# Two decoder layers at batch 8: the layer norm taken off the chain between attention and feed-forward, and two visits instead of four placed between the layers

## The chip, the cores and the metric

The kernel runs on one core of one Trainium2 chip. The metric is the time of one execution on the device in microseconds (us); of several executions the median counts. Beside the times there is one execution taken by the hardware profiler, with its own time and its span (first to last instruction).

The engines are called PE (matmul; PEld is its weight load), DVE (vector), ACT (scalar activation), POOL (GpSimd) and SP, the engine whose queue issues all the DMAs here.

## The reference

Eight sequences decode one token each (D = 640). The same attention block and the same feed-forward block are applied twice, with the same weights and the same cache:

```python
x = A_x
x = x + _A_ref(_layernorm(x), k_cache, v_cache, wq, wo)
x = x + _B_ref(_layernorm(x), w1, w2)
x = x + _A_ref(_layernorm(x), k_cache, v_cache, wq, wo)
x = x + _B_ref(_layernorm(x), w1, w2)
```

`_A_ref` is attention with 32 heads of 128 over 4096 cached positions: q = x wq, scores q.k / sqrt(128), softmax, weighted sum of v, output projection wo. `_B_ref` is relu(x w1) w2 with 1728 hidden values. `_layernorm` is (x - mean) / sqrt(var + 1e-5) without weights. Everything is bfloat16. The cache is 8 x 32 x 4096 x 128 elements each for keys and values, 1.07 GB together.

## The kernel before, in words

**Tiles.** A *visit* is one sequence b with one pair of heads hp in one layer: (layer, b, hp). It needs the keys of the pair (K) and its values (V), each in four *units* of 128 partitions x 2048 bf16, 512 KB. The units live in an *arena* of G = 26 places. SP loads one to eight neighbouring units with one DMA (`do_load`, L477).

**Order of the work.** `plan` (L33) writes the whole program out beforehand, as a list of steps. For each sequence it runs 16 visits of layer 0 and, later, 16 of layer 1. The last three pairs of heads in layer 0 are the first three in layer 1, and 21 of their units stay in the arena (`keep`, L59); two more are copied to PSUM and back (`stash`, L60; `do_stash` L464, `do_unstash` L472). So 23 units of a sequence are loaded once instead of twice. Between the last visit of layer 0 of sequence b and its first visit of layer 1 the plan puts the first AHEAD = 4 visits of sequence b + 1 (L43 to L49), since layer 1 can't begin before the feed-forward block is through. While those visits run, the 21 kept units are held and five places are left.

Within the list, K of a visit comes before V of the visit ahead of it (L63 to L65); at the end of a sequence's layer 0 the two are swapped. `feed` (L106) puts a load into the list as soon as places are free, so SP's queue follows the order in which PE frees units (`release`, L137). A load waits on SP until the matmuls that read the old unit are done. Everything else is a *chain*: a list of steps with costs, from which `step` (L159), called after each unit, takes one step of each chain as long as the costs stay within CAP = 20. `until` (L168) runs a chain forward to a step that is needed now. The engines' queues follow this list in order; nothing is reordered later.

**One visit.** Scores: 64 matmuls with the cache as weights (L524). Then the row maximum (M1, L530), across partitions (T L534, M2 L538, B L543), exponentials on ACT (E, L545: a maximum with the scale -1/sqrt(128), and Exp with the scale 1/sqrt(128)), sums (L556, I), the product with V (L512), its copy on ACT (OC, L570), gathering (OG, L575), division by the sum (O, L585), output projection with 10 matmuls (W, L592), and the addition to x on DVE (Y, L601). Layer 1 does W for all eight sequences at once, at the end.

**The end of a layer** (`finish`, L178, and `finish_steps`, L404). After Y of the last visit the chain has these steps: sums of x over its five columns (DVE), mean (a fp32 matmul with ones), center (subtract, square, reduce, on DVE), var (a fp32 matmul), scale. In layer 0, scale calls `inverse_root` (L386): one operation on DVE and eleven on POOL, then one more on POOL (L375) that writes the normalized row. Two empty steps follow. Then come five steps `up` (70 matmuls with w1, L417), relu on ACT (L425, L428), five steps `down` (70 matmuls with w2, L434), add. In layer 0 the same norm follows for layer 1, and then the queries of the first two pairs (Q L496, QC on ACT L504); each further query is made two visits ahead. Layer 1's end, done once for all sequences, takes the root with Sqrt on ACT (L380) and a reciprocal on DVE instead.

The pieces of the plan that set this:

```python
visits += nxt[:AHEAD] + cur + nxt[AHEAD:]
norm = [(0, "sums"), (2, "mean"), (0, "center"), (2, "var"), (0, "scale"), (1, None), (1, None)]
c = norm + [(15, ("up", k)) for k in range(n_up)] + [(0, "relu")]
c += [(14, ("down", k)) for k in range(n_down)] + [(0, "add")]
if layer == 0:
    c += norm
```

Of the kernel before, what the change touches and what calls it, by code (L numbers as in the profile page):

```python
# [16 lines left out]
UNIT = 4  # L17
# [5 lines left out]
AHEAD = 4  # L23
# [9 lines left out]
def plan(B, NP, n_up, n_down):  # L33
# [29 lines left out]
    for i in range(NV + 1):  # L63
        pair = [("K", i)] * (i < NV) + [("V", i - 1)] * (i >= 1)
        slots += pair[::-1] if i and visits[i - 1][0] == 0 and last_of[visits[i - 1][:2]] == i - 1 else pair  # L65
    stream = []
    for which, i in slots:
        layer, b, hp = visits[i]
        stream += [(which, i, g) for g in range(UNIT) if layer == 0 or (which, hp, g) not in keep]
# [7 lines left out]
    weights.setdefault(max(1, NP - 4), []).append(("w2",))  # L77

# [16 lines left out]
    def place(x):  # L95

        if visits[x[1]][0] and stashed(*x) is not None:
            return None, stashed(*x), False
        return visits[x[1]][1], tile_at(NP, x[0], visits[x[1]][2]) * UNIT + x[2], keeps(*x)
# [6 lines left out]
    def feed():  # L106

        while at[0] < len(stream):
# [4 lines left out]
            while n < most and b is not None and place(stream[at[0] + n]) == (b, p + n, keeping):  # L113
                n += 1
# [10 lines left out]
            if b is None:  # L125
                lands[u] = clock[0] + 2
                ops.append(("unstash", p, u))
                continue
# [8 lines left out]
    def release(which, i, g):  # L137
        key = which, visits[i][1], visits[i][2], g
        u = where.pop((which, i, g), None)
        if key in kept:  # L140
            if visits[i][0] == 0:
                return
            u = kept.pop(key)
        if visits[i][0] == 0 and stashed(which, i, g) is not None:
            ops.append(("stash", stashed(which, i, g), u))
        at[1] += 1
        owner[u], freed[u] = False, at[1]
        feed()
# [29 lines left out]
    def finish(layer, b):  # L178

        norm = [(0, "sums"), (2, "mean"), (0, "center"), (2, "var"), (0, "scale"), (1, None), (1, None)]  # L180
        c = norm + [(15, ("up", k)) for k in range(n_up)] + [(0, "relu")]
        c += [(14, ("down", k)) for k in range(n_down)] + [(0, "add")]
        if layer == 0:
            c += norm
        c = [(n, op and ("C", layer, b, k, op)) for k, (n, op) in enumerate(c)]
        if layer == 0:
            c += query(b, 0) + query(b, 1)
# [3 lines left out]
    for which, i in slots:  # L191
# [18 lines left out]
        if which == "K":  # L210
            ops.append(("M1", i))
# [3 lines left out]
        else:  # L215
            until(("I", i))
            ops.append(("OC", i))
            step()
            chains.append([(6, ("OG", i)), (0, ("O", i))])
            if layer == 0 or b == B - 1:  # L220
                chains[-1] += [(10, ("W", i)), (0, ("Y", i))]
            if last_of[layer, b] == i and (layer == 0 or b == B - 1):
                chains[-1] += finish(layer, b)
# [16 lines left out]
def kernel(  # L240
# [82 lines left out]
    for c in range(4):  # L323
        rows = slice(32 * c, 32 * c + CJ)
        nc.vector.tensor_copy(out=gsel[rows, :, c // 2], in_=ident[rows, rows])
    eps_c = consts.tile([P, 1], FP32, name="eps_c")
# [19 lines left out]
    def ln_steps(b0, nb, xln, key):  # L346
        x = xT[:, b0 : b0 + nb, :]

        def sums():
            s1 = st[key, "s1"] = sm.tile([P, nb], FP32, name="s1", bufs=1)  # L350
            nc.vector.tensor_reduce(out=s1, in_=x, axis=AX.X, op=ALU.add)

        def mean():
            st[key, "mean"] = oy_ps[:, 64 : 64 + nb]
            nc.tensor.matmul(st[key, "mean"], lhsT=ones_f, rhs=st[key, "s1"], start=True, stop=True)

        def center():
            xc = st[key, "xc"] = sm.tile([P, nb, DC], FP32, name="xc", bufs=1)
            nc.vector.scalar_tensor_tensor(
                out=xc, in0=_free(st[key, "mean"], [(1, nb), (0, DC)]), scalar=-1.0 / D, in1=x, op0=ALU.mult, op1=ALU.add  # L360
            )
            sq = sm.tile([P, nb, DC], FP32, name="sq", bufs=1)
            nc.vector.tensor_tensor(out=sq, in0=xc, in1=xc, op=ALU.mult)
            s2 = st[key, "s2"] = sm.tile([P, nb], FP32, name="s2", bufs=1)
            nc.vector.tensor_reduce(out=s2, in_=sq, axis=AX.X, op=ALU.add)

        def var():
            st[key, "var"] = oy_ps[:, 72 : 72 + nb]
            nc.tensor.matmul(st[key, "var"], lhsT=ones_f, rhs=st[key, "s2"], start=True, stop=True)

        def scale():
            rstd = sm.tile([P, nb], FP32, name="rstd", bufs=1)
            if nb == 1:
                inverse_root(rstd, st[key, "var"])
                nc.gpsimd.tensor_scalar(  # L375
                    out=xln[:, 0, :], in0=st[key, "xc"][:, 0, :], scalar1=rstd, scalar2=None, op0=ALU.mult
                )
            else:
                std = sm.tile([P, nb], FP32, name="std", bufs=1)
                nc.scalar.activation(out=std, in_=st[key, "var"], func=ACT.Sqrt, bias=eps_c, scale=1.0 / D)  # L380
                nc.vector.reciprocal(out=rstd, in_=std)
                nc.vector.tensor_tensor(out=xln, in0=st[key, "xc"], in1=_free(rstd, [(1, nb), (0, DC)]), op=ALU.mult)

        return dict(sums=sums, mean=mean, center=center, var=var, scale=scale)

    def inverse_root(out, s2):  # L386
# [3 lines left out]
        nc.vector.tensor_scalar(out=v[:, 0:1], in0=s2, scalar1=1.0 / D, scalar2=eps, op0=ALU.mult, op1=ALU.add)  # L390
# [12 lines left out]

    def finish_steps(layer, b):  # L404


        b0, nb = (b, 1) if layer == 0 else (0, B)
        xf = sm.tile([P, nb, DC], BF16, name="xf", bufs=1)
        key = layer, b

        def up(k):
            if k == 0:
                st[key, "h"] = oy_ps[:, 128 : 128 + FC * nb].rearrange("p (f b) -> p f b", b=nb)
            for f in up_parts[k]:
                fs = f_sizes[f]
                for c in range(DC):
                    nc.tensor.matmul(  # L417
                        st[key, "h"][:fs, f, :], lhsT=w1_sb[:, c, f * P : f * P + fs], rhs=xf[:, :, c],
                        start=(c == 0), stop=(c == DC - 1),
                    )  # L420

        def relu():
            hT = st[key, "hT"] = sm.tile([P, FC, nb], BF16, name="hT", bufs=1)
            if n_full:
                nc.scalar.activation(out=hT[:, :n_full], in_=st[key, "h"][:, :n_full], func=ACT.Relu)  # L425
            if Dff % P:
                rem = Dff % P
                nc.scalar.activation(out=hT[:rem, n_full:], in_=st[key, "h"][:rem, n_full:], func=ACT.Relu)  # L428

        def down(c):  # L430
            if c == 0:
                st[key, "y"] = oy_ps[:, 256 : 256 + DC * nb].rearrange("p (c b) -> p c b", b=nb)
            for f, fs in enumerate(f_sizes):
                nc.tensor.matmul(  # L434
                    st[key, "y"][:, c, :], lhsT=w2_sb[:fs, f, c * P : (c + 1) * P],
                    rhs=st[key, "hT"][:fs, f, :], start=(f == 0), stop=(f == FC - 1),
                )

        def add():
            dst = xT if layer == 0 else outT  # L440
            nc.vector.tensor_tensor(
                out=dst[:, b0 : b0 + nb, :], in0=xT[:, b0 : b0 + nb, :],
# [229 lines left out]
```

## Time and profile before

| what | value |
|---|---|
| time, median of 3 runs | 2374.44 us (2373.16 to 2378.14) |
| the profiled execution's own time | 2376.09 us |
| its span | 2374.3 us, 57948 instructions |
| busy: PE, PEld | 1292.5 us (54%), 783.7 us (33%) |
| busy: DVE, ACT, POOL | 377.7 us (16%), 355.9 us (15%), 42.8 us (2%) |
| moved by DMA | 996.04 MB, mean 420 GB/s |
| read from HBM | 992.27 MB |
| loads of the cache | 632 DMAs: 348 of 1 unit, 35 of 2, 17 of 3, 100 of 4, 16 of 5, 6 of 6, 1 of 7, 109 of 8 |

How to read the profile: the page gives the busy time of each engine, then the span in 40 slices with DMA share and rate, then the chain of waits followed back from the last instruction, then groups of instructions and the DMA issues with their time from issue to landing. A view by stages gives the same figures for any stretch of the span; a timeline lists the instructions in order, with, in brackets, how long the engine was idle before each and what released it. The DMA share is the time in which packets were under way on the core's 16 DMA engines.

### The profile page before, as it was taken

How to read it: one execution, taken by the hardware profiler on the slowest of the kernel's cores; microseconds unless marked ns; L12 is line 12 of the kernel's file. 1: busy time of each engine (PE TensorE's matmuls, PEld its weight loads, DVE VectorE, ACT ScalarE, POOL GpSimd, SP SyncE). 2: the span in 40 equal slices, each digit the busy share in tenths (PEclk: the TensorE clock that was granted, in tenths of full speed). 3: DMA queues.
4: the chain of work that ended last, by engine and by line, in shares of the span. 5: the costliest groups of instructions: out<-in, count | busy, mean ns of one | idle time of the engine just before them, and what ended most of it. 6: DMA issues, size and time to landing. Idle time of an engine off the chain costs nothing.

```text
span 2374.3 us, 57948 instructions
## 1 busy us (share of the span) xinstructions
PE 1292.5 (54%) x26486; PEld 783.7 (33%) x26486; DVE 377.7 (16%) x1840; ACT 355.9 (15%) x1195; POOL 42.8 (2%) x198
## 2 busy tenths in 40 slices
PE   3436644476445754458454574446744466545845
PEld 2324322243223532225222352223422244223523
DVE  1102111121111211112111121112211112112211
ACT  1111211111111211112111121111211112111211
POOL 0000000000000000000000000000000000000000
DMA  9999999999999999999999999999999999999997
GB/s 411 428 429 403 428 432 431 429 398 433 428 433 427 391 433 428 433 423 404 430 434 433 406 401 431 433 431 408 420 431 430 430 408 417 431 432 410 405 434 302
DMA packets 92794, 996.04 MB, mean 420 GB/s; under 512 B 10372, under 2 KB 10372, under 8 KB 54916
## 3 DMA queue, kind: packets, MB, share of 16 engines
q1 hardware_dynamic: 92548, 992.33, 99.1%
q8 instruction: 207, 3.39, 0.5%
q14 instruction: 39, 0.32, 0.0%
HBM read 992.27 MB, written 0.01 MB: 418 GB/s over the span
## 4 chain that ended last, share of the span: by engine, by line
DMA 81%; PE 14%; DVE 2%; ACT 2%; issue 1%; POOL 1%; SPq 0%; POOLq 0%; DVEq 0%; ACTq 0%
DMA arena<-in_A_kv_dram 81%; PE o_ps L512 5%; PE s_ps L524 5%; ACT o_sb L570 1%; DVE hmx L538 1%; PE oy_ps L575 1%; PE blk_ps L496 1%; PE blk_ps L543 1%; DVE diag L540 0%; PE oy_ps L592 0%; PE blk_ps L534 0%; PE oy_ps L434 0%; DMA wq_sb<-in_A_wq_dram 0%; DVE arena L475 0%; POOL root L399 0%
## 5 line engine op out<-in xcount | busy, mean ns | idle before, releaser
L512 PE MATMUL o_ps<-arena,P_sb 128*4 128x512 bf16 x4096 | 564.8, 599 | 373.9 <-DMA arena<-in_A_kv_dram 371.6
L524 PEld LDWEIGHTS <-arena 128*128 128x128 bf16 x16384 | 501.6, 105 | 667.0 <-DMA arena<-in_A_kv_dram 660.7
L524 PE MATMUL s_ps<-q_96,arena 128*128 128x1 bf16 x8192 | 275.2, 166 | 371.9 <-DMA arena<-in_A_kv_dram 360.0
L547 ACT ACTIVATE nmax<-blk_ps 128x2 f32<-128x2 f32 x256 | 44.0, 172 | 1638.3 <-PE blk_ps L543 1638.3
L512 PEld LDWEIGHTS <-P_sb 128*4 128x4 bf16 x4096 | 90.6, 81 | 442.5 <-issue 429.4
L570 ACT CAST o_sb<-o_ps 100x512 bf16<-100x512 f32 x256 | 149.8, 585 | 228.8 <-PE o_ps L512 228.8
L562 DVE TENSOR_REDUCE lsum<-blk_ps 128x2 f32<-128x64 f32 x256 | 57.3, 224 | 588.6 <-PE blk_ps L556 588.6
L530 DVE TENSOR_REDUCE mrow<-s_ps 128x2 bf16<-128x64 f32 x256 | 57.5, 224 | 578.1 <-PE s_ps L524 542.6
L551 ACT ACTIVATE P_sb<-s_ps,nmax 128x32 bf16<-128x32 f32 x512 | 118.8, 283 | 8.2
L538 DVE TENSOR_REDUCE hmx<-blk_ps 2x1 f32<-2x128 f32 x256 | 71.4, 279 | 207.2 <-PE blk_ps L534 207.2
L556 PEld LDWEIGHTS <-onesb_c 128*128 128x128 bf16 x256 | 26.4, 103 | 199.7 <-issue 199.7
L585 DVE TENSOR_TENSOR oT<-oy_ps,invL 128x2 bf16<-128x2 f32 x128 | 20.4, 160 | 350.5 <-PE oy_ps L575 350.5
L575 PE MATMUL oy_ps<-gsel,o_sb 100*128 100x2 bf16 x1024 | 66.1, 168 | 17.5 <-ACT o_sb L570 0.7
L534 PE MATMUL blk_ps<-ident,mrow 128*2 128x128 bf16 x256 | 70.0, 274 | 3.1 <-DVE mrow L530 3.1
L543 PEld LDWEIGHTS <-onesb_c 2*128 2x128 bf16 x256 | 25.1, 98 | 125.1 <-issue 125.0
L556 PE MATMUL blk_ps<-P_sb,onesb_c 128*128 128x64 bf16 x256 | 59.7, 233 | 0.0
L575 PEld LDWEIGHTS <-o_sb 100*128 100x128 bf16 x1024 | 47.4, 106 | 33.6 <-ACT o_sb L570 29.6
L524 PE MATMUL s_ps<-q_22833,arena 128*128 128x1 bf16 x1024 | 34.1, 166 | 43.6 <-DMA arena<-in_A_kv_dram 43.4
L524 PE MATMUL s_ps<-q_18821,arena 128*128 128x1 bf16 x1024 | 33.9, 166 | 43.4 <-DMA arena<-in_A_kv_dram 43.3
L524 PE MATMUL s_ps<-q_2773,arena 128*128 128x1 bf16 x1024 | 33.9, 166 | 42.7 <-DMA arena<-in_A_kv_dram 42.7
L524 PE MATMUL s_ps<-q_14809,arena 128*128 128x1 bf16 x1024 | 34.1, 166 | 42.4 <-DMA arena<-in_A_kv_dram 41.9
L524 PE MATMUL s_ps<-q_10797,arena 128*128 128x1 bf16 x1024 | 33.9, 166 | 42.6 <-DMA arena<-in_A_kv_dram 42.5
(179 smaller groups left out, 781.2 us busy)
## 6 DMA issues: line engine op xcount, KB each, us to landing
arena<-in_A_kv_dram SPq DMA_DIRECT2D x109, 4096.0 KB, 24.8
arena<-in_A_kv_dram SPq DMA_DIRECT2D x100, 2048.0 KB, 25.2
arena<-in_A_kv_dram SPq DMA_DIRECT2D x348, 512.0 KB, 6.2
arena<-in_A_kv_dram SPq DMA_DIRECT2D x16, 2560.0 KB, 22.6
arena<-in_A_kv_dram SPq DMA_DIRECT2D x35, 1024.0 KB, 12.8
arena<-in_A_kv_dram SPq DMA_DIRECT2D x17, 1536.0 KB, 24.4
arena<-in_A_kv_dram SPq DMA_DIRECT2D x6, 3072.0 KB, 23.3
wq_sb<-in_A_wq_dram SPq DMA_DIRECT2D x4, 1280.0 KB, 30.0
```

The source lines that it names most:

```text
L512: nc.tensor.matmul(o_ps[32 * c : 32 * c + CJ, :], lhsT=P_tiles[i][:, h, j : j + CJ], rhs=arena[:, at + c * CJ * Dh : at + (c + 1) * CJ * D ...
L524: nc.tensor.matmul(s_tiles[i][:, j : j + 1], lhsT=arena[:, at + n * P : at + (n + 1) * P], rhs=q, start=True, stop=True)
L530: nc.vector.tensor_reduce(out=m_tiles[i], in_=s_tiles[i].rearrange("p (h j) -> p h j", h=2), axis=AX.X, op=ALU.max)
L534: nc.tensor.matmul(blk[i][:2, :P], lhsT=m_tiles.pop(i), rhs=ident, start=True, stop=True)
L538: nc.vector.tensor_reduce(out=hmx, in_=blk[i][:2, :P], axis=AX.X, op=ALU.max)
L543: nc.tensor.matmul(blk[i][:, P : P + 2], lhsT=ones_b, rhs=nmax.pop(i), start=True, stop=True)
L547: nc.scalar.activation(out=nm, in_=blk[i][:, P : P + 2], func=ACT.Copy, scale=-inv_sqrt_dh)
L551: nc.scalar.activation(out=P_tiles[i][:, h, :], in_=S[:, h, :], func=ACT.Exp, bias=nm[:, h : h + 1], scale=inv_sqrt_dh)
L556: nc.tensor.matmul(blk[i][:, P + 2 :], lhsT=ones_p, rhs=P_tiles[i].rearrange("p h j -> p (h j)"), start=True, stop=True)
L562: nc.vector.tensor_reduce(out=L, in_=blk.pop(i)[:, P + 2 :].rearrange("p (h j) -> p h j", h=2), axis=AX.X, op=ALU.add)
L570: nc.scalar.copy(out=o_tiles[i][:OR], in_=o_ps[:OR, :].rearrange("p (j d) -> p j d", j=CJ))
L575: nc.tensor.matmul(oy[i][:, :2], lhsT=o_tiles[i][:OR, j, :], rhs=gsel[:OR, j, :], start=(j == 0), stop=(j == CJ - 1))
```

## The change

1. **Mean from column sums of wo.** Ahead of the end of a layer's attention, the sum of x over its columns is taken before the last visit's output is added (S). The mean of the new x is then the sum of that with the last visit's o times the column sums of wo. `do_ws` makes these column sums once, for the two pairs of heads that close a layer, as a bf16 value and a bf16 rest. W then carries five more matmuls.
2. **YC** takes the place of Y, sums, mean and center at that place: it centres x with the mean and adds the last visit's output, first as the bf16 input of the feed-forward block.
3. **The root after the product.** The feed-forward block starts on the centred row without the scale; var and root come after the second `up` step, and relu, now on DVE, multiplies by the root: max(h, 0) x rstd. Layer 1's queries are made from the centred row, and the root enters in the scale of the scores, which E reads from a tile `q_scale` (with the factor 1/sqrt(128) in it).
4. **Two visits ahead**, not four; at the turn to layer 1, V of the last visit comes before K of the first kept one.
5. **The stash** isn't part of the stream of loads any more; it comes back SOON = 4 units before its use.
6. Queries of even and odd pairs have a place of their own in PSUM.

```diff
-AHEAD = 4
+SOON = 4
+AHEAD = 2
...
-        slots += pair[::-1] if i and visits[i - 1][0] == 0 and last_of[visits[i - 1][:2]] == i - 1 else pair
+        ends = i and visits[i - 1][0] == 0 and last_of[visits[i - 1][:2]] == i - 1
+        turns = 0 < i < NV and visits[i][0] == 1 and visits[i - 1][0] == 0
+        slots += pair[::-1] if ends or turns else pair
...
-        stream += [(which, i, g) for g in range(UNIT) if layer == 0 or (which, hp, g) not in keep]
+        uses += [(which, i, g) for g in range(UNIT)]
+        stream += [(which, i, g) for g in range(UNIT) if layer == 0 or (which, hp, g) not in keep | set(stash)]
...
+        x = uses[at[1] + SOON] if at[1] + SOON < len(uses) else None
+        if x and visits[x[1]][0] and stashed(*x) is not None:
+            u = where[x] = room(1)
+            owner[u] = True
+            lands[u] = clock[0] + 2
+            ops.append(("unstash", stashed(*x), u))
...
-        norm = [(0, "sums"), (2, "mean"), (0, "center"), (2, "var"), (0, "scale"), (1, None), (1, None)]
-        c = norm + [(15, ("up", k)) for k in range(n_up)] + [(0, "relu")]
-        c += [(14, ("down", k)) for k in range(n_down)] + [(0, "add")]
+        for k in range(n_up):
+            c += [own(15, "up", k)]
+            if k == min(1, n_up - 1):
+                c += [own(0, "var"), own(0, "root")]
+        c += [own(0, "relu")] + [own(14, "down", k) for k in range(n_down)] + [own(0, "add")]
         if layer == 0:
-            c += norm
+            c += [own(2, "mean"), own(0, "center")] + query(b, 0)
+            c += [own(1, "var2"), own(0, "root2")] + query(b, 1)
...
+            if layer and hp == order1[0]:
+                until(("C", 0, b, "root2"))
             ops.append(("M1", i))
...
+            if i == NP - 2:
+                ops.append(("WS", closing))
             chains.append([(6, ("OG", i)), (0, ("O", i))])
+            if last_of[layer, b] == i and (layer == 0 or b == B - 1):
+                chains[-1] += [(0, ("S", i)), (16, ("W", i)), (0, ("YC", i))] + finish(layer, b)
...
+    def do_ws(closing):
+        for n, hp in enumerate(closing):
+            ws = sm.tile([P, 2], FP32, name="wsum", bufs=1)
+            nc.vector.tensor_reduce(out=ws, in_=wo_sb[:, 2 * hp : 2 * hp + 2, :], axis=AX.X, op=ALU.add)
+            nc.vector.tensor_copy(out=wo_sum[:, n, 0, :], in_=ws)
+            nc.vector.tensor_tensor(out=wo_sum[:, n, 1, :], in0=ws, in1=wo_sum[:, n, 0, :], op=ALU.subtract)
...
+        nc.vector.scalar_tensor_tensor(
+            out=xc, in0=_free(st.pop("sum"), [(1, nb), (0, DC)]), scalar=-1.0 / D, in1=x, op0=ALU.mult, op1=ALU.add
+        )
+        xf = st["xf"] = sm.tile([P, nb, DC], BF16, name="xf", bufs=1)
+        nc.vector.tensor_tensor(out=xf, in0=xc, in1=y, op=ALU.add)
+        nc.vector.tensor_tensor(out=xc, in0=xc, in1=y, op=ALU.add)
+        nc.vector.tensor_tensor(out=x, in0=x, in1=y, op=ALU.add)
+        st["s2"] = squares(xc)
...
-                nc.scalar.activation(out=hT[:, :n_full], in_=st[key, "h"][:, :n_full], func=ACT.Relu)
+                    nc.vector.scalar_tensor_tensor(
+                        out=hT[:rows, fs], in0=h[:rows, fs], scalar=0.0,
+                        in1=_free(st["rstd"][:rows], [(0, fs.stop - fs.start), (1, nb)]), op0=ALU.max, op1=ALU.mult,
+                    )
...
+            r = q_scale[b] = sm.tile([P, 2], FP32, name="q_scale", bufs=2)
+            inverse_root(r[:, 0:1], oy_ps[:, 72:73], float(Dh))
+            nc.gpsimd.tensor_scalar(out=r[:, 1:2], in0=r[:, 0:1], scalar1=-1.0, scalar2=None, op0=ALU.mult)
...
+        less, more = (q_scale[b][:, 1:2], q_scale[b][:, 0:1]) if layer else (-inv_sqrt_dh, inv_sqrt_dh)
+        nc.scalar.activation(out=nm, in_=blk[i][:, P : P + 2], func=ACT.Copy, scale=less)
...
+        if "sums" in st:
+            st["sum"] = oy_ps[:, 64 : 64 + nb]
+            nc.tensor.matmul(st["sum"], lhsT=ones_f, rhs=st.pop("sums"), start=True, stop=False)
+            for n in range(4):
+                nc.tensor.matmul(
+                    st["sum"], lhsT=_free(wo_sum[:, layer, n // 2, n % 2 : n % 2 + 1], [(0, P)]),
+                    rhs=o1[:, 2 * hp + n % 2, :] if layer else oT[i][:, n % 2 : n % 2 + 1], start=False, stop=(n == 3),
+                )
```

## The prediction

> **What bounds the kernel now.** First the page: its rows of DMA share and rate, the DMA queues, and the chain of work that ended last.
>
> ```profile
> DMA  9999999999999999999999999999999999999997
> GB/s 411 428 429 403 428 432 431 429 398 433 428 433 427 391 433 428 433 423 404 430 434 433 406 401 431 433 431 408 420 431 430 430 408 417 431 432 410 405 434 302
> ...
> q1 hardware_dynamic: 92548, 992.33, 99.1%
> ...
> DMA 81%; PE 14%; DVE 2%; ACT 2%; issue 1%; POOL 1%; SPq 0%; POOLq 0%; DVEq 0%; ACTq 0%
> ```
>
> The DMA engines are never idle and 81% of the chain is cache loads, so the time is bytes divided by rate, plus a start and a tail. The rate isn't even: it is 428 to 434 GB/s, with a dip in every fourth or fifth slice. Eight dips are the eight ends of layer 0. Next the stages, around the second dip (columns: stretch, length, busy time of PE, PEld, DVE, ACT, POOL, clock, DMA share, GB/s).
>
> ```profile
> 543.00:767.00 224.00, 107.60 (x2205) 61.82 (x2201) 32.32 (x155) 30.91 (x106) 0.00 (x0) 1.00 1.00 431
> ...
> 479.00:497.00 18.00, 12.68 (x245) 8.19 (x243) 3.33 (x19) 2.44 (x8) 2.63 (x12) 1.00 0.97 380
> 497.00:515.00 18.00, 14.78 (x290) 10.37 (x288) 3.67 (x20) 2.68 (x10) 1.47 (x7) 1.00 1.02 410
> 515.00:533.00 18.00, 13.51 (x304) 8.81 (x301) 4.37 (x19) 5.01 (x14) 1.16 (x5) 1.00 1.02 402
> 533.00:543.00 10.00, 9.51 (x203) 5.44 (x199) 2.48 (x13) 2.76 (x10) 0.00 (x0) 1.00 1.03 423
> ```
>
> Between the ends the rate is 431. At an end, while 21 of the arena's 26 units are kept for layer 1, it is 380, 410 and 402 in three stretches of 18 us, then 423. The DMA share stays near 1: packets merely take longer, so the share doesn't show the loss, the rate does. Over all eight ends the three stretches have 383, 380, 376, 381, 368, 373, 381, 373 (mean 377), then 411, 410, 404, 410, 380, 415, 407, 381 (mean 402), then 404, 402, 382, 400, 387, 403, 388, 400 (mean 396). The DMA issues say what differs there:
>
> ```profile
> arena<-in_A_kv_dram SPq DMA_DIRECT2D x109, 4096.0 KB, 24.8
> arena<-in_A_kv_dram SPq DMA_DIRECT2D x348, 512.0 KB, 6.2
> ```
>
> At an end loads are one unit of 512 KB. Five units are left to turn over: a load lands 6.2 us after issue, PE reads it for about 0.6 us, and only then is the next issued. Five units in 6.8 us would be 386 GB/s; the loop is just at the edge of the queue's rate, so whatever delays PE there shows in the rate.
>
> **What the Trainium skill says.** "DMA: Bandwidth & Descriptors", section on the anatomy of one DMA: about 2.0 us fixed, most of it completion, plus bytes over 436e3. That gives 3.2 us for a unit; the trace's 6.2 us is longer, because the unit also queues behind up to four others. So the loop has some slack, an estimate of 6.2 - 0.6 - 3.2 = 2.4 us. The same page, "Where 436 GB/s comes from", puts the fabric at 435; the quiet stages' 431 agree, so there is no faster stage in which a lost microsecond could be won back.
>
> **The change, part by part.** The sum is made against the profiled execution: span 2374.3 us, its own time 2376.09, which is 1.65 above the median 2374.44. Savings are taken off the median.
>
> *Two visits between layers, not four.* In the built plans the bytes are the same (1864 units), but loads of one unit fall from 348 to 235 (29 at an end where 43 stood), and loads of eight rise from 109 to 127. So 14 units per end, 7.34 MB, move to quiet stages. At the middle stretch's 402 GB/s they are 18.2 us: the middle stretch itself drops out. Its loss is 18 x (1 - 402/431) = 1.20 us, times 8 = **9.6 us**.
>
> *The first stretch* loses 18 x (1 - 377/431) = 2.26 us. The order of SP's loads up to it is unchanged, and it begins when the arena fills up. I book no saving, though a norm's waits leave it: that is an upside of up to 0.8 us per end, 6 us in all, and the downside is rival two.
>
> *The third stretch* loses 18 x (1 - 396/431) = 1.46 us. At the fourth's rate of 423 it would be 0.33. Between the two lie the second root, which the first query matmul waits for, and two unstashes, which take two of the five units early. The timeline of POOL gives the root of the first end:
>
> ```profile
> 223.48 0.19 POOL L391 TENSOR_SCALAR root<-root 128x1 int32<-128x1 int32 x1 [16.19 <-DVE root L390]
> ...
> 226.70 0.31 POOL L375 TENSOR_SCALAR xq<-xc,rstd 128x5 bf16<-128x5 f32 x1
> ```
>
> That is 3.5 us in which no query can start. After the change queries need only the centred row, and the root is read first by the softmax of the first layer 1 visit, some six matmul groups later; the unstash comes four uses ahead. I take half the excess, (1.46 - 0.33)/2 = 0.57, times 8 = **4.6 us**; bounds 0 and 9.
>
> *What the end issues now.* Dropped ahead of the FFN: the waits for the mean, the variance, the root and POOL's scaling; ahead of the queries, the root and the other scaling. The mean's fp32 matmul (0.56 us for its two passes) moves up behind W's ten, with four bf16 ones of about 0.04, thus 0.7 us on PE; then come six DVE operations of 0.16 to 0.17, where five were, and only the first two precede the FFN. They lie beside the next unit's wait for DMA (PE waited for DMA before most units here). If that cover is gone, 1 us per end, 8 in all. The root (11 POOL operations, 3.2 us) has three units of 1.25 us until relu needs it: even. Relu goes to DVE, two operations of about 0.2 where ACT had 0.18 and 0.16; behind it on DVE waits only the row maximum of the next visit.
>
> *The column sums (WS)*, once: a reduce costs 0.16 us at 5 elements and 0.224 at 64, about 1.1 ns each, so two of 1280 are 2.9 us, with four small ones 3.5 us. Queued behind them on DVE is O of visit 14, on which W, PE and so the last units of V wait; two units (2 x 0.8 us) cover part. I take **+1.2 us**, bounds 0 and 3.
>
> *The tail.* From the timeline at the end:
>
> ```profile
> 2361.64 0.41 PE L592 MATMUL oy_ps<-o_97,wo_sb 128*128 128x8 bf16 x10 [0.26 <-DVE o_97 L585]
> ...
> 2365.42 2.26 PE L417 MATMUL oy_ps<-xf,w_sb 128*128 128x8 bf16 x70 [0.83 <-DVE xf L382]
> ```
>
> From the end of W (2362.05) to the FFN is 3.37 us. It becomes the sum matmuls (0.76) and two DVE operations of 0.20 with hand-offs, 1.3 us: 2.1 saved. The var matmul (0.60) now lies inside the FFN product, and relu's two DVE operations over 104 and 8 columns (0.27 and 0.2) take 0.2 more than ACT's pair. Net **1.3 us**. The activation table of 1.28 us, already beside W, stays so.
>
> Sum: 9.6 + 4.6 + 1.3 - 1.2 = 14.3, so 2374.4 - 14.3 = **2360 us**.
>
> **The rivals.** *One, all dips shrink:* PE's waits cause them all, and without two of them the first and third stretches run at the fourth's rate but for the arena filling. 9.6 + 9 + 6 = 24.6, less what WS takes beside the tail: 2350. For it: in the first stretch the first FFN product waits for the POOL root. Against it: the first stretch is low from its first microseconds on, before any root. Chance 0.08.
>
> *Two, the waits only move:* the same 16 chain steps now lie in 16 units where 28 stood, so stalls that the middle stretch held recur in the other two, and only the price of a small load's packets is saved, 14 units x (0.524/423 - 0.524/431), 0.023 us each, 2.6 us in all. With tail and WS: 2372. For it: each of the 16 gaps between units holds one step, with none to spare. Chance 0.17.
>
> *Three, slower: PE becomes the bound of the short window.* Place: PE's queue from the first K unit after the last V of layer 0 to the first kept K. Price: the 16 units at 1.25 us give it 20 us. Before, PE is busy 25.5 us in 36 there (198 to 234); twelve units (0.6 each) and some visit work (2 us) leave, about 16.5 us stay. If waits between engines in so full a queue add 7.5 us, the window takes 4 us more per end: 32 - 14 = 18, 2392. It decides from 1.8 us more per end (14.3/8). Against it: the densest stretch of the kernel before shows that such a queue doesn't hurt:
>
> ```profile
> 1657.00:1675.00 18.00, 15.54 (x305) 11.12 (x305) 3.83 (x21) 2.67 (x10) 2.03 (x10) 1.00 1.03 415
> ```
>
> PE is busy 86% of it, and its rate is the best of the eight. Chance 0.09.
>
> **How the numbers follow.** The main case has 0.66 and by itself 2352 to 2367. The range of 2350 to 2372 takes in rivals one and two and leaves out three and some of the edges. A measurement of this kernel tells about 0.2%, 4.7 us, from no change. Faster by more: the main case, rival one and a part (0.07) of two: 0.81. Within: the rest of two and a part (0.02) of three: 0.12. Slower: 0.07.
>
> **What would show it.** At each end the low rates should last about 40 us rather than 58, with 29 loads of one unit; the first stretch still near 377, the next above 396, and no wait of a query matmul for POOL. The second FFN product should start about 1.3 us sooner after the last W. It would be wrong if the dips got deeper as they got shorter, if PE waits for DVE's relu appear before the second FFN product at every end, or if WS holds V's last units for more than 3 us.

## The result, and the profile after

| | before | after |
|---|---|---|
| time, median | 2375.02 us of 4 runs (2373.16 to 2378.14) | 2387.73 us of 4 runs (2385.31 to 2390.05) |
| ratio, 95% interval | | 1.0052 [1.0035, 1.0069] |
| span of the profiled execution | 2374.3 us | 2388.2 us |

The change made the kernel slower by about half a per cent. The forecast was 2360, with a range that ended at 2372. First the page of the kernel after: its rate in 40 slices, the queue of the loads, and the chain that ended last.

```profile
GB/s 409 426 426 392 429 427 430 426 385 430 429 429 424 397 428 427 433 420 398 431 427 430 405 412 428 427 431 403 416 428 428 427 398 414 427 430 426 392 429 308
...
q1 hardware_dynamic: 78724, 992.32, 98.9%
...
DMA 77%; PE 16%; ACT 3%; DVE 2%; issue 1%; POOL 0%; SPq 0%; POOLq 0%; DVEq 0%; ACTq 0%
```

The bytes are those of before (992.32 and 992.33 MB), in fewer packets, and DMA still bounds the kernel. Two things differ in the rate. The dips are deeper in their worst slice (385 where 391 was the lowest), and the slices between them, in which nothing was changed, stand mostly at 426 to 430 where they stood at 428 to 434. The view by stages says it for the quiet stretch after the second end and for that end (columns as in the prediction).

```profile
550.00:760.00 210.00, 98.12 (x2015) 58.82 (x2014) 27.38 (x138) 29.89 (x94) 0.00 (x0) 1.00 1.00 429
```

```profile
482.00:500.00 18.00, 14.34 (x307) 9.89 (x307) 3.57 (x21) 2.25 (x8) 1.46 (x7) 1.00 0.95 365
500.00:518.00 18.00, 14.87 (x298) 10.78 (x299) 3.81 (x23) 2.38 (x10) 3.36 (x16) 1.00 1.00 368
518.00:536.00 18.00, 16.30 (x359) 10.20 (x356) 5.28 (x23) 7.75 (x21) 0.00 (x0) 1.00 1.03 416
536.00:546.00 10.00, 6.94 (x125) 3.49 (x121) 2.03 (x10) 3.14 (x9) 0.00 (x0) 1.00 1.00 421
```

The low stage did get shorter: 365 and 368 for 36 us, then 416, where 380, 410 and 402 had filled 54. But 36 us at 366 lose more than 54 us at 397: 36 x (1 - 366/431) = 5.4 us against 54 x (1 - 397/431) = 4.3 us. Dips that get deeper as they get shorter were the first thing that the prediction named as a sign of being wrong.

To add this up I count, from the packets, the loss of a stretch as its length less its bytes over a rate. An *end* is the 64 us from the first one-unit packet, the rest is quiet.

```
                      before    after
quiet rate, GB/s      430.42    427.96
loss of 8 ends, us     40.05     41.35   (each against its own quiet rate)
last packet to end     15.13     13.89
```

Of the 13.9 us that the span grew, the lower quiet rate takes 1799 us x (430.42/427.96 - 1) = 10.3 in the quiet stages and 512 us x the same = 2.9 in the ends; the ends add 1.3 of their own; the tail gives back 1.2 (what is missing, 0.6, lies in the first and the last loads). Most of the loss thus lies where the change moved no instruction. The cause had to be something that touches every load.

What differs for every load is where it lands. The tile `wo_sum`, 16 bytes a partition, was put ahead of the weights and the arena (its line isn't among the pieces of the diff shown above; it is the first line of the diff in the next section). With it the arena begins at byte 119072 of a partition in the built program instead of 119040: the 16 bytes move it by 32. 119040 is a multiple of 256; 119072 is 32 past it. The median packet of 16 KB took 614 ns after and 611 before, of 32 KB 1216 and 1213, of 8 KB 313 and 309: 3 or 4 ns each, whether the packet is short or long. Only the packets of 4 KB, those of the one-unit loads, have the same median of 159 ns in both.

**Theories.** The first: the address of the arena slows every packet, and the change proper is a gain hidden beneath it. Its rival: the new work at the ends (relu on DVE, the root's scale in ACT, a fuller PE queue in the short window, which is the prediction's third rival) is what costs. A third, on why the gain proper is smaller than forecast: with five places the loop of one-unit loads has no slack.

### The profile page after: what moved, and what is told of

It is laid out like the page before. It is cut to its first block, busy times and chain, and to the rows that moved or that the text cites. A ratio compares the mean times of both kernels' runs of the same rounds, so it can differ in the third digit from the quotient of the medians.

```text
span 2388.2 us, 57845 instructions
## 1 busy us (share of the span) xinstructions
PE 1281.9 (54%) x26522; PEld 792.0 (33%) x26522; DVE 383.6 (16%) x1889; ACT 386.2 (16%) x1177; POOL 39.3 (2%) x190
## 3 DMA queue, kind: packets, MB, share of 16 engines
q1 hardware_dynamic: 78724, 992.32, 98.9%
## 4 chain that ended last, share of the span: by engine, by line
DMA 77%; PE 16%; ACT 3%; DVE 2%; issue 1%; POOL 0%; SPq 0%; POOLq 0%; DVEq 0%; ACTq 0%
DMA arena<-in_A_kv_dram 77%; PE s_ps L575 7%; PE o_ps L563 4%; ACT P_sb L604 2%; DVE hmx L589 1%; PE blk_ps L547 1%; PE oy_ps L628 1%; ACT nmax L600 1%; PE blk_ps L594 1%; PE oy_ps L450 1%; PE oy_ps L645 1%; PE blk_ps L585 1%; PE blk_ps L609 1%; DVE diag L591 0%; ACT o_sb L623 0%
## 5 line engine op out<-in xcount | busy, mean ns | idle before, releaser
L575 PEld LDWEIGHTS <-arena 128*128 128x128 bf16 x16384 | 495.2, 104 | 443.8 <-DMA arena<-in_A_kv_dram 418.2
L575 PE MATMUL s_ps<-q_97,arena 128*128 128x1 bf16 x8192 | 272.9, 166 | 313.7 <-DMA arena<-in_A_kv_dram 308.1
L563 PEld LDWEIGHTS <-P_sb 128*4 128x4 bf16 x4096 | 95.7, 82 | 710.7 <-issue 692.2
L600 ACT ACTIVATE nmax<-blk_ps 128x2 f32<-128x2 f32 x128 | 22.0, 172 | 1051.5 <-PE blk_ps L594 1051.5
L600 ACT ACTIVATE nmax<-blk_ps,q_scale 128x2 f32<-128x2 f32 x128 | 33.6, 262 | 652.7 <-PE blk_ps L594 650.5
L604 ACT ACTIVATE P_sb<-s_ps,nmax,q_scale 128x32 bf16<-128x32 f32 x256 | 82.6, 373 | 4.3
L604 ACT ACTIVATE P_sb<-s_ps,nmax 128x32 bf16<-128x32 f32 x256 | 59.4, 283 | 4.1
L594 PE MATMUL blk_ps<-diag,onesb_c 2*128 2x2 bf16 x256 | 41.7, 163 | 25.8 <-DVE diag L591 0.4
L575 PE MATMUL s_ps<-q_30433,arena 128*128 128x1 bf16 x1024 | 34.5, 166 | 38.3 <-DMA arena<-in_A_kv_dram 37.4
L547 PE MATMUL blk_ps<-xq,wq_sb 128*128 128x1 bf16 x1280 | 52.2, 165 | 3.0 <-DVE hmx L589 2.6
```

What stands on the lines that cost most here:

```text
L547: nc.tensor.matmul(q_ps[:, h : h + 1], lhsT=wq_sb[:, g, c, (2 * n + h) * Dh : (2 * n + h + 1) * Dh], rhs=xlns[b][:, 0, c : c + 1], start=( ...
L563: nc.tensor.matmul(o_ps[32 * c : 32 * c + CJ, :], lhsT=P_tiles[i][:, h, j : j + CJ], rhs=arena[:, at + c * CJ * Dh : at + (c + 1) * CJ * D ...
L575: nc.tensor.matmul(s_tiles[i][:, j : j + 1], lhsT=arena[:, at + n * P : at + (n + 1) * P], rhs=q, start=True, stop=True)
L594: nc.tensor.matmul(blk[i][:, P : P + 2], lhsT=ones_b, rhs=nmax.pop(i), start=True, stop=True)
L600: nc.scalar.activation(out=nm, in_=blk[i][:, P : P + 2], func=ACT.Copy, scale=less)
L604: nc.scalar.activation(out=P_tiles[i][:, h, :], in_=S[:, h, :], func=ACT.Exp, bias=nm[:, h : h + 1], scale=more)
```

## The experiments

Ratios are against the kernel before, timed on the same chip.

**The arena back on its address.** The kernel after with `wo_sum` behind the arena instead of ahead of it.

```diff
-    wo_sum = consts.tile([P, 2, 2, 2], BF16, name="wo_sum")
...
     arena = kv.tile([P, G * GW], BF16, name="arena")
+    wo_sum = kv.tile([P, 2, 2, 2], BF16, name="wo_sum")
```

> The changed kernel, with the 16-byte tile wo_sum moved from ahead of the weights and the arena to behind them; nothing else is changed. In the built program the arena then starts at byte 119040 of a partition, as before the change, and not at 119072. Theory A (the shifted address makes each packet some 4 ns longer, and this is what slows the stages between the ends of layer 0 from 430.4 to 428.0 GB/s): those stages return to 430.4 and some 10 us are won, about 2377. Theory B (the lower rate is another chip's or another allocation in HBM, or comes from something else in the change): no change, about 2388.

Measured: 2367.66 us, ratio 0.9974 [0.9966, 0.9982]. The view by stages of this kernel, quiet stretch and second end:

```profile
550.00:760.00 210.00, 98.78 (x2072) 60.17 (x2069) 27.45 (x139) 29.22 (x91) 0.00 (x0) 1.00 1.00 431
```

```profile
478.00:496.00 18.00, 14.22 (x306) 9.89 (x302) 3.40 (x20) 2.45 (x8) 2.23 (x11) 1.00 0.95 378
496.00:514.00 18.00, 14.65 (x296) 10.53 (x295) 3.81 (x23) 3.13 (x12) 2.60 (x13) 1.00 1.01 384
514.00:532.00 18.00, 17.09 (x342) 9.63 (x341) 5.70 (x25) 7.63 (x21) 0.00 (x0) 1.00 1.03 427
532.00:542.00 10.00, 7.17 (x180) 5.20 (x176) 1.77 (x9) 2.50 (x8) 0.00 (x0) 1.00 1.01 428
```

No instruction was removed, yet 20 us are gone: the quiet stretch is back at 431, every stretch of the end is 7 to 16 GB/s higher than after, and the packets are back at 309, 611 and 1213 ns. The times of all packets, added up and divided by the 16 engines, are 2356.5 us here and 2375.7 us after: 19 of the 22 us between the two profiled spans (2365.8 and 2388.2). This version beats both kernels. What is left of the change proper is a gain of 0.26%, 6.2 us.

**The shift alone.** The kernel before with an unused tile of 16 bytes ahead of the weights.

```diff
+    pad = consts.tile([P, 8], BF16, name="pad")
+    nc.vector.memset(pad, 0.0)
     eps_c = consts.tile([P, 1], FP32, name="eps_c")
```

> The kernel before the change, with an unused 16-byte tile put ahead of the weights and the arena, so that the arena starts at byte 119072 and not at 119040. Theory A: the stages between the ends fall to about 428 GB/s and the time rises by some 10 to 13 us, to about 2386. Theory B: no change, about 2375.

Measured: 2393.6 us, ratio 1.0088 [1.0073, 1.0102]. The quiet stretch of this kernel:

```profile
550.00:760.00 210.00, 101.98 (x2109) 59.26 (x2109) 28.04 (x141) 28.48 (x98) 0.00 (x0) 1.00 1.01 428
```

A tile that nobody reads costs more than the whole change did. Both directions agree: from after to its aligned form 20 us by the medians and 18.5 by the ratios, from before (2374.36 us on that chip) to its shifted form 19 and 21. Both moved by more than was expected (10 us, and 10 to 13), since the expectations priced the quiet stages alone.

**Which addresses are slow.** The same with tiles of 64, 128 and 256 bytes (`[P, 32]`, `[P, 64]`, `[P, 128]` in the diff above). The letters of the theories are those of these three runs alone.

> The kernel before with an unused tile of 64 bytes a partition ahead of the weights and the arena: the arena begins at byte 119104, 64 past a multiple of 256. Theory A, a load's packets are slow whenever the arena does not begin on a multiple of 256 bytes: as with the tile of 16 bytes, 2393 us, quiet stages 427.6 GB/s, packets of 16 KB with a median of 614 ns. Theory B, it is the start within 64 bytes that counts: 2374, as before, 430.4 GB/s, 611 ns. Theory C, not the address but one tile and one operation more at the start: 2393 here and in the two runs beside it.

> The same with 128 bytes: the arena begins at byte 119168, 128 past a multiple of 256. Theory A: 2393 us and 427.6 GB/s. Theory B, and a rule of 128 bytes: 2374 us and 430.4 GB/s. Theory C: 2393.

> The same with 256 bytes: the arena begins at byte 119296, again a multiple of 256, while the tile and its operation at the start stay. Theories A and B: 2374 us, as before, 430.4 GB/s and 611 ns for a packet of 16 KB. Theory C: 2393.

Measured, with the runs above beside them:

```
arena past a multiple of 256   time     ratio [interval]          quiet   16 KB packet of the cache, median / mean
0    before                    2375.02                            430.4   611 / 613.0 ns
32   16-byte tile              2393.60  1.0088 [1.0073, 1.0102]   427.5   614 / 617.7
64   64-byte tile              2391.23  1.0082 [1.0068, 1.0096]   428.1   613 / 616.7
128  128-byte tile             2385.38  1.0069 [1.0056, 1.0081]   428.3   613 / 616.3
0    256-byte tile             2369.63  0.9998 [0.9990, 1.0006]   430.5   611 / 613.0
```

The tile of 256 bytes and its operation cost nothing (before took 2371.46 us on that chip), so it isn't the tile (theory C falls); 64 and 128 are slow, so it isn't a start within 64 bytes (theory B falls). Theory A holds: at the three offsets tried off a multiple of 256 the loads are slow. The mean packet is a little less slow at 128 than at 32, which A didn't say; the intervals of the times overlap. The packets also lose their uniformity: in the kernel before, 99% of the 16 KB packets took the same 611 ns, while with the 16-byte tile they spread from 612 to 621. The 207 fetches of instructions, packets of 16 KB that don't land in the arena, grow too, from a median of 935 ns to 1069 to 1073 in all slow kernels. Spread over 16 engines that is under 2 us of the 20; why they grow wasn't tested. The weights in front of the arena were shifted with it, and no kernel shifted the arena alone; but the weights are loaded once, and what is loaded all the time is the arena.

**Is it the new work?** Two kernels in the aligned form. The first gives layer 1's scores the constant scale back:

```diff
-        less, more = (q_scale[b][:, 1:2], q_scale[b][:, 0:1]) if layer else (-inv_sqrt_dh, inv_sqrt_dh)
+        less, more = -inv_sqrt_dh, inv_sqrt_dh
```

> The kernel of e1, with constants as the scale of the exponentials in layer 1 too: it leaves the root of the second norm out of the scores. It takes away what the scale read from a tile costs ACT (0.26 for 0.17 us and 0.65 for 0.46 us in each visit of layer 1). Theory P (PE waits for the exponentials while the kept units are read, and that holds up the loads): the ends lose some 0.5 us less each, 4 us in all against e1. Theory D (the ends are lost by PE's own queue while the two visits between the layers run): within 1 us of e1, since the loads are ahead by then.

Measured: 2368.37 us, 0.9978 [0.9970, 0.9985], as the aligned form. The scale from a tile does lengthen ACT; the view of the tile nmax in the aligned form shows both kinds (minimum, median and maximum in ns):

```profile
L604 ACT ACTIVATE P_sb<-s_ps,nmax x256: 278/284/288, 24.3 to 2196.1; 128x32 bf16<-128x32 f32 x128
L604 ACT ACTIVATE P_sb<-s_ps,nmax,q_scale x256: 367/374/378, 224.6 to 2348.0; 128x32 bf16<-128x32 f32 x128
L600 ACT ACTIVATE nmax<-blk_ps x128: 172/172/173, 22.8 to 2195.7; 128x2 f32<-128x2 f32 x128
L600 ACT ACTIVATE nmax<-blk_ps,q_scale x128: 262/262/264, 224.3 to 2347.4; 128x2 f32<-128x2 f32 x128
```

That is 90 ns for each, a cost that the prediction overlooked (the Trainium skill has it: "ScalarE: Activation LUTs", the section on the cost of ACT_TABLE_LOAD, gives about 93 ns for a pointer operand; the trace agrees). 128 x 0.09 + 256 x 0.09 = 35 us of ACT time, all of it beside the loads: without it the kernel is no faster, as theory D said.

The second lightens PE in the short window: layer 0's feed-forward block with one matmul for each sum.

```diff
-                for c in range(DC):
+                for c in range(DC if layer else 1):
...
+            n_f = FC if layer else 1
-            for f, fs in enumerate(f_sizes):
+            for f, fs in enumerate(f_sizes[:n_f]):
```

> The kernel of e1, with only the first of five matmuls for each tile of the first FFN product and the first of fourteen for each of the second in layer 0: it leaves out most of the FFN's sums there, 121 of 140 matmuls at each end, and keeps every step and every wait between engines. Theory D (PE's queue is so full in the short window that each unit is read late, and with five units in turn every delay is a gap in the loads): the ends lose 1 to 2 us less each, some 8 to 14 us in all against e1. Theory L (the loop of five units is bound by the fixed time of a load and by the bubble at its beginning, PE's work apart): within 2 us of e1.

Measured: 2366.67 us, 0.9973 [0.9962, 0.9983]. With 121 of 140 matmuls gone at every end, PE is busy for 28 us less over the eight ends (397 us of 512 where it was 425), and the time is 1 us off the aligned form's, which can't be told from nothing. So PE's load of matmuls isn't what limits the short window; the waits between the engines, which this kernel keeps, aren't tested by it. The prediction's third rival wanted 18 us lost with two visits; the aligned form, which has them, is faster than the kernel before. It falls, although its sign was the one that came.

**More places.** The aligned form with six and with seven places free at the ends, so that one or two kept units less save a load.

```diff
-SPARE = 5
+SPARE = 6
```

> The kernel of e1, with six free places at an end of layer 0 in place of five: one unit less is kept, so eight units more are loaded in all (1872, not 1864; 8 x 0.524 MB at 430.6 GB/s are 9.7 us). Theory L (a unit is seen by PE some 3.4 us after its last packet, so that five places turn over just as fast as the queue moves data, with 0.4 us to spare, and each small delay is a gap): with a sixth place there is 1.6 us to spare, the ends lose 15 to 20 us less than e1's 33, and the time is 2358 to 2363. Theory F (the gaps come from what the queue itself does there, the fetches of instructions and the short packets): the ends lose about as before, and the time rises by the bytes, to about 2377.

> The kernel of e1, with seven free places at an end in place of five: sixteen units more are loaded (1880; 19.5 us). Theory L: the ends lose little more than the price of short packets, 5 to 10 us in all, so 2360 to 2366, no better than e5. Theory F: about 2387.

Measured: 2369.62 us, 0.9982 [0.9976, 0.9989], and 2379.10 us, 1.0019 [1.0010, 1.0028]. Both times lie between the two theories, and neither number came. 8 and 16 more units of 524 KB cost 9.7 and 19.5 us at 431 GB/s, but by the ratios the kernels are only 1.9 and 10.7 us slower than the aligned form. So the ends gained some 8 and 9 us; the profiled executions give 6.4 and 7.2 (a loss of 33.4 us at the eight ends falls to 27.0 and 26.2). Places matter, though the second one bought almost nothing: lack of places is a part of the loss at the ends, not all of it.

**The parts apart.** First the aligned form with four visits between the layers (`AHEAD = 4`), then the kernel before with two (`AHEAD = 2`).

> The kernel of e1, with four visits between the layers again: of the change only the norm's part and the order of the stash remain. If the shorter window is what wins (theory S), the ends lose as much as before the change, 40 us, and the time is about 2373, the tail's 1.3 us apart. If the norm's part wins (theory N), it stays at about 2368.

> The kernel before the change, with two visits between the layers and the norm where it was. The chain's last steps don't fit into the sixteen units and are run in one go ahead of the first query: down's remaining four steps, the norm and its root on POOL, some 7 us in which PE reads no unit. Theory S (the window's length alone matters): about 2369. Theory N (two visits need the shorter chain): 5 to 7 us of stall at each of eight ends, less the window's gain, so 2405 to 2425.

Measured: 2372.80 us, 0.9995 [0.9988, 1.0001], and 2435.65 us, 1.0263 [1.0249, 1.0277]. The rest of the change with four visits is worth nothing that can be told, as theory S said; two visits with the old norm lose 62 us, more than the 30 to 50 that theory N gave them. The view by stages and that of PE's waits show how the latter loses, at the second end:

```profile
514.00:532.00 18.00, 12.15 (x275) 8.01 (x274) 4.64 (x21) 5.03 (x15) 2.63 (x12) 1.00 0.61 211
```

```profile
PE blk_ps L496 <- POOL xq L375: 3.9, 1, 3.9
```

The old chain doesn't fit into two visits: the query waits 3.9 us for POOL's root and scaling, PE frees nothing meanwhile, and the DMA share falls to 0.61, some 7 us of 18 and most of the 7.8 us that an end loses. So the shorter chain's worth is that it lets the window be cut; the cut itself (four visits against two, the rest of the change in both) is worth (0.9995 - 0.9974) x 2374 = 5.0 us. The two intervals don't overlap; together they leave an estimate of 2.5 us either way. The order at the turn, the stash and the places of the queries (points 4 to 6 of the change) weren't tried one by one.

**Where the ends lose.** From the packets, in us for one end, mean of eight, against 431 GB/s; times counted from the first one-unit packet:

```
                            8-16    16-64   0-64
before                      1.75    3.15    5.08
before, 256-byte tile       1.62    2.43    4.25
after                       1.95    3.29    5.58
aligned, four visits        1.69    2.55    4.43
aligned                     1.63    2.41    4.23
aligned, light product      1.66    2.19    4.04
aligned, six places         1.55    1.58    3.42
aligned, seven places       0.49    2.71    3.30
```

The first two rows are the same plan, and differ by 0.8 us an end: one profiled execution tells the loss of eight ends to some 6 us, no better. For amounts I therefore use the timed ratios. But one thing stands in nearly all: 1.6 to 2 us are lost from 8 to 16 us after the first one-unit packet. (The prediction called the first stretch low from its first microseconds on; in the kernel before, its first 8 us run at 408 to 421 GB/s at every end.) In the aligned form's fourth end the view by stages resolves it:

```profile
1059.00:1063.00 4.00, 3.38 (x40) 1.09 (x37) 0.71 (x4) 1.22 (x4) 0.00 (x0) 1.00 1.01 407
1063.00:1067.00 4.00, 2.51 (x56) 1.80 (x52) 0.23 (x2) 0.58 (x1) 0.00 (x0) 1.00 0.86 319
1067.00:1071.00 4.00, 3.63 (x101) 3.35 (x101) 1.66 (x10) 0.00 (x0) 0.67 (x4) 1.00 1.01 378
```

Between the issues at 1058.5 and 1065.3 SP issues no load, since what PE reads then are kept units, which free no place. The five units in flight run out, the DMA share drops to 0.86, and 4 x (1 - 319/431) = 1.0 us is gone in four. (0.14 x 4 us is 3% of 18 us: the share of 0.97 in the first stretch, which the prediction passed over with "the share doesn't show the loss", was this gap.) It is there in before as well (no issue between 192.5 and 199.3), and the change doesn't touch it. Seven places put it later and remove it only at the first end.

## Why the prediction was wrong

**The term that was missing.** "In the built plans the bytes are the same", and so each byte was taken to cost the same. It didn't: +20 us by the address of the arena (2387.73 - 2367.66; 18.5 by the ratios). This term, put at nothing without a reason, is the step that turned a gain into a loss. None of the rivals had it; the prediction looked at instructions, queues and waits, and not at where a new tile puts its neighbours. The whole diff has the tile, and its place ahead of the arena could have been seen beforehand. Without the term the number would have come into the range, at 2368, but not by the sum that was made: of its two largest terms one was half as large and the other can't be found.

What the Trainium skill states would have been a reason to look. "DMA: Bandwidth & Descriptors", section on how a descriptor splits into AXI transactions, says that a descriptor that doesn't start on 256 bytes has its first transaction begin at the boundary below, at the cost of extra beats. It tells this of bytes that are fetched; here the side that was shifted is the one written to. The direction agrees. The size doesn't follow beats: of the 512 beats of 32 bytes in a 16 KB packet each takes 611/512 = 1.2 ns, so that offsets of 32, 64 and 128 bytes would add an estimated 1.2, 2.4 and 4.8 ns; measured are 3, 2 and 2 in the median and 4.7, 3.7 and 3.3 in the mean, which fall where the beats rise. "SBUF — State Buffer", section on operand start alignment, treats what is allowed and says that its runs "timed nothing"; here the time is what the address changed. That the mechanism is the split was not shown, only that offsets of 32, 64 and 128 bytes are slow and one of 256 isn't.

**Two visits, not four (9.6 us booked).** Measured by the pair of kernels above: 5.0. The step "the middle stretch itself drops out" failed by half. Its loss didn't vanish with its 14 loads; the second stretch runs at 390 GB/s in the aligned form in the mean of the eight ends (384 at the second), where it had 402 (410) in the kernel before and more than 396 was forecast. That fits rival two ("the waits only move"), in part of its size; that it is these waits that hold the rate down wasn't shown.

**The third stretch (4.6 booked).** The rate there rose, to 427 in the aligned form where 402 stood, but this is no longer the same work: the shorter window is over by then, and the second root and the queries lie in the stretch before (POOL has no operation in the line of 514 to 532, x0). The fair comparison is the aligned form with four visits, where the window still covers it. Its second end:

```profile
498.00:516.00 18.00, 13.47 (x249) 9.11 (x248) 4.13 (x24) 2.77 (x10) 2.52 (x12) 1.00 1.02 399
516.00:534.00 18.00, 11.09 (x212) 6.92 (x213) 2.22 (x12) 1.97 (x6) 0.00 (x0) 1.00 1.03 414
```

In the mean of the eight ends its third stretch has 414 GB/s where the kernel before had 396; but the same plan as before, in the kernel with the 256-byte tile, has 408, so up to two thirds of this difference can be the scatter of single executions. The timed gain isn't there: the ratio is 0.9995, 1.2 us, and the tail alone is worth that. In the kernel after, the queries don't wait for the root, as predicted (at 221.46 and 222.40 they run while POOL's second root goes from 221.30 to 224.71); nothing that can be timed came of it. So the wait for the root, on which half of the excess was booked, cost next to nothing; what made the stretch slow isn't shown.

**The loop's slack.** I took 2.4 us of slack from the Trainium skill's 2.0 us and bytes over 436e3 ("DMA: Bandwidth & Descriptors", anatomy of one DMA). That section gives the sum for DMAs that GpSimd issues; these are issued by SP. The shortest landing of a one-unit load in the trace of before is 5.2 us, not 3.2. (From a unit's last packet to its landing the median is 1.5 us there, between 0.2 and 4.0; the 3.4 us in the expectation for six places doesn't come out of the trace.) Five places turning over at 1.25 us are 6.25 us; with 5.2 of landing and 0.6 of reading, less than half a us is left by this estimate. It isn't a fixed price, since in it a load still queues behind others: one landed in 4.2 us in the aligned form, which would leave 1.5. The prediction's own 386 GB/s, for five units in 6.8 us, had left none. With little slack a delay at any of the steps can show in the rate, and fewer loads in the window hold the same number of steps; the gain from a sixth place speaks for this. The median landing after answers to the 6.2 us of before:

```profile
arena<-in_A_kv_dram SPq DMA_DIRECT2D x127, 4096.0 KB, 25.1
...
arena<-in_A_kv_dram SPq DMA_DIRECT2D x235, 512.0 KB, 6.8
```

The counts, 235 and 127, are those forecast; the landing got longer, in the aligned form too (6.5).

**The column sums, relu and the root.** The timeline of the first end after:

```profile
195.96 1.47 DVE L411 TENSOR_REDUCE wsum<-wo_sb 128x2 f32<-128x1280 bf16 x1
...
197.86 1.49 DVE L411 TENSOR_REDUCE wsum<-wo_sb 128x2 f32<-128x1280 bf16 x1
...
199.87 0.40 PE L645 MATMUL oy_ps<-oT,wo_sb 128*128 128x1 bf16 x10 [2.29 <-DVE oT L638]
...
209.18 0.19 POOL L404 TENSOR_TENSOR rstd<-root 128x1 f32<-128x1 f32 x1
...
209.54 0.23 DVE L469 SCALAR_TENSOR_TENSOR hT<-oy_ps,rstd 128x13 bf16<-128x13 f32 x2 [2.45 <-PE oy_ps L450]
```

The estimate of 1.45 us for a reduce was right, and W waited 2.29 us, under the 3 that I had named as a limit. The 1.2 us booked can't be found: in the aligned form the first stretch of this end has 379, of the second 378. The root (done at 209.37) isn't what relu waits for at this end; the bracket names PE's product. "Even" was right here.

**The tail (1.3 booked).** Right: 1.24 us less from the last packet to the end. The timeline:

```profile
2376.64 0.41 PE L645 MATMUL oy_ps<-o_98,wo_sb 128*128 128x8 bf16 x10 [0.26 <-DVE o_98 L638]
...
2377.33 0.25 PE L653 MATMUL oy_ps<-o_98,wo_sum 128*128 128x8 bf16 x4
...
2378.44 0.95 PE L450 MATMUL oy_ps<-xf,w_sb 128*128 128x8 bf16 x30 [0.86 <-DVE xT L434]
...
2382.02 0.49 PE L476 MATMUL oy_ps<-hT,w_sb 128*128 128x8 bf16 x13 [0.42 <-DVE hT L469]
```

From the end of W, 2377.05, to the first product are 1.39 us (3.37 before, 1.3 predicted), and to the second 4.97 (6.02 before: 1.05 sooner, 1.3 predicted).

**The sum.** Booked -14.3. Measured: tail -1.2, window -5.0, nothing else that can be told, thus -6.2 in the aligned form; and, by the ratios, +18.5 for the address. 2375.0 - 6.2 + 18.5 = 2387.3, where 2387.7 was measured.

**What stays open.** Why the loop of the short window still loses some 2.4 us an end after the gap at its beginning, with PE's matmuls of the feed-forward block and the tile's scale on ACT ruled out, and why a second more place doesn't help as the first did. Fetches of instructions (16 KB each, 0.94 us) fall into it; but between 16 and 40 us the lightened product has two of them in most ends where the aligned form has three, and loses about as much, so they aren't shown to be the cause. What mechanism makes a packet longer off 256 bytes was not tried.

## What to carry to other kernels

Before predicting a change that adds a tile, work out where it moves the buffers that the DMAs fill: here 16 bytes ahead of the arena cost three times what the change gained, and moving the tile behind the arena brought it back. If stages that a change doesn't touch change their rate, look for something that all their instructions share before explaining the stages that it does touch. A stretch with a low rate may not be booked as saved when it is cut out while the chain of steps that lay in it stays: here half of the booked loss remained. And a rate of one stretch in one execution scatters: the same plan had 396 and 408 GB/s in its third stretch.

## What the runs showed of the hardware

- Packets of 8, 16 and 32 KB that land 32, 64 or 128 bytes past a multiple of 256 in SBUF take 2 to 4 ns longer in the median (4 KB: none to 1); the quiet rate goes from 430.4 to between 427.5 and 428.3 GB/s, and a kernel of 2374 us bound by such loads grows by 0.7 to 0.9%. At 256 bytes past it nothing changes (ratio 0.9998).
- A scale from a tile instead of a constant costs ACT 90 ns an instruction (172 to 262 ns, 284 to 374 ns).
- The first product after the change waits for the addition to x (DVE xT, L434), although its own input (xf, L432) was complete at 2378.05, 0.39 us earlier. The addition is the last to read the PSUM tile oy_ps, which the product writes; that this is why it waits is a reading of the kernel, not a test.
